# Routed attention and a token/channel mixer on one core: half sums of the exponentials added on VectorE, denominators a unit later, and another row for the stored weights

## The chip, the cores and the metric

The kernel runs on one core of a Trainium2 chip. The core has a matrix engine (TensorE, PE in the profile, with its weight loads shown as PEld), VectorE (DVE), ScalarE (ACT), GpSimd (POOL) and SyncE (SP), which here only issues transfers. Transfers are carried by 16 DMA engines. Working data lies in one SBUF tile named `arena`; TensorE writes into PSUM, the tile `ps` of eight banks. The metric is the time of one execution in microseconds on the device. Before the change its median is 799.9 us over three runs, which lay between 799.69 and 800.42.

## The reference

Everything is float32. Attention comes first, with 4 batches, 8 heads, 768 tokens and 64 values per head; a token sees only the tokens whose nearest centroid (of 16 for its head) is its own:

```python
q_assign = argmax(einsum('bhsd,hcd->bhsc', q_n, c_n), -1)   # the same for k
mask = q_assign[:, :, :, None] == k_assign[:, :, None, :]
scores = where(mask, scale * q @ k.T, -1e9)
attn = exp(scores - max(scores));  attn = attn / (sum(attn) + 1e-9)
x = (attn @ v)  # as (B, S, H*D) = (4, 768, 512)
```

Then a mixer over tokens and one over channels:

```python
h = maximum(x.T @ w_tok1, 0) @ w_tok2;   u = x + h.T
out = u + maximum(u @ w_ch1, 0) @ w_ch2    # 512 -> 1536 -> 512
```

The four weight matrices come as 8-byte floating point numbers, and the kernel itself turns them into float32.

## The kernel before

**The planner.** The program is not issued as it is written. Each operation is added to a `Program` (L74) with the engines that can do it, an estimated cost, and what it reads and writes. `run` (L117) gives each one a due time, worked back from the times at which PE would want its results, and `plan` (L148) then orders every engine's instructions: PE keeps the order in which its work was added, the other engines take, of what is ready, whatever is due first. `after` is the earliest time the plan may start an operation. The estimated costs stand in `COST` (L52) and the latency of transfers in `add` and `plan`. What comes out is a fixed order per engine; every engine then works in that order and waits for semaphores where it must. SP issues nearly all transfers, in one queue.

**Attention.** The 32 heads are done as 16 pairs. `pair(m)` (L1283) first runs `scores(m)` (L1148): twelve chunks, each of two score products (64 rows of the array each) plus two small products that add the mask, into two of the banks 0 to 5, and for each chunk one exponential on ACT (L1191) over 768 columns. The results lie in six buffers of a ring of seven (`exs`), each 128 x 1536. Then come the products with v (`values`, L1219, six per pair, each 16 small matrix products 32 columns wide) into banks 6 and 7, `route(m + 2, 0)` for a later pair's mask, and `sums(m, 5)` (L1233), which adds up the denominators over partitions.

The denominators are made in two steps. VectorE adds the six buffers by threes: two sums `es[0]` and `es[1]`, two adds each, every one of them 128 x 1536 (end of `scores`). Then `sums` multiplies both by a matrix of ones, four small products of 384 columns for each of the two, one accumulating onto the other in bank 5. `finish_x` (L1247) transposes the denominators out of bank 5 (L1250), keeps them in `dall`, takes reciprocals, transposes the products out of banks 6 and 7 (L1264) and multiplies. In PE's order `sums(m)` stands ahead of the last of the six `values` of the same pair.

Beside this, q and k are loaded, split into 16-bit halves by ACT (`part_qk`), transposed by DMA, and joined again by ACT (`join_qk`, L871).

**Weights.** During attention VectorE also rounds the weights from 8 bytes, in 31 pieces of up to 512 columns: `weight_round` (L1307), four instructions (L1327 to L1337) and an add. Piece n may be loaded from 14 + 11 n us of the plan on. `channel_weights` (L1384) handles the two big matrices: per slice s two pieces fill the first four of eight operands in `O`, VectorE makes the other four with `sub1`, and four more per slice with `sub2` into `Os`. These are the seven weight forms of Strassen's scheme in Winograd's variant, at two levels, which trades matrix products for additions. Seven stores per slice write them to scratch tensors in DRAM, `wd1` and `wd2`, in rows of 256 bytes (64 values), 224 KB each.

**Mixer.** The token stage (`token1`, `token2`) makes `uTs`, with VectorE adding each PE result of 384 columns. Then for each of two groups of batches `channel1` and `channel2` run seven products (`product`, L1671), each of seven weight forms. A weight form is 192 KB, loaded from `wd1` or `wd2` into one of eight `ring` buffers in rows of 1536 bytes, and used by three matrix products of 128 x 384. `weights_in_range` and `check` (L1872) count what tells whether a slower, more careful path would be needed (it isn't). `check` is written between the two groups: eight short VectorE instructions and a small matrix product.

Of the kernel before, what the change touches and what calls it, by code (L numbers as in the profile page):

```python
# [20 lines left out]
P = 128  # L21
# [28 lines left out]
GRAIN = 32  # L50

COST = {  # L52
    "ACT": (0.09, 0.00083),
    "ACT16": (-0.36, 0.001426),
# [12 lines left out]
START, STEP = 14, 11  # L67


class Op:  # L70
    __slots__ = ("opts", "fn", "preds", "succs", "left", "ready", "end", "due", "seq", "eng", "lat", "bytes", "after", "port", "first_lat", "mode", "early")


class Program:  # L74
# [10 lines left out]
    def add(self, opts, fn, rd=(), wr=(), size=None, after=0.0, mode=None, early=0.0):  # L85
# [3 lines left out]
        o.lat, o.mode, o.early = 0.0, mode, early  # L89

        o.port = not any(type(k) is tuple and k[0] == "ps" for k in list(rd) + list(wr))
        if size:
            o.bytes = BUS * size[0] / size[1] * (11 + 0.037 * size[1]) / 16e3
            o.lat = 5.0 + o.bytes / BUS
# [53 lines left out]
    def plan(self):  # L148
# [14 lines left out]
        while len(order) < len(ops):  # L163
# [39 lines left out]
            if o.bytes:  # L203
                bus = max(bus, o.end + 0.6) + o.bytes / BUS
                o.lat = bus + LAND - o.end
# [514 lines left out]
def kernel(  # L720
# [36 lines left out]
    wd1 = dram.tile([7, 7, P, 3 * P], F32, name="wd1")  # L757
    wd2 = dram.tile([7, 7, P, 3, P], F32, name="wd2")
# [45 lines left out]
    O = buf(119, [8, 2, 2, W])  # L804
# [62 lines left out]
    def halves(dst, src, n, rd, wr, engines=("ACT",)):  # L867

        def fn(e):
# [6 lines left out]
            {e: cost("ACT16" if e == "ACT" else e, n) for e in engines}, fn, rd, wr  # L876
# [17 lines left out]
    def vec(fn, c, rd, wr, early=0.0):  # L894
        return g.add({"DVE": c - 0.08}, lambda e: fn(), rd, wr, early=early)
# [8 lines left out]
    def transpose(dst, src, rd, wr, kb):  # L904
        return g.add(
            {"SP": ISSUE}, lambda e: nc.sync.dma_start(dst, src, transpose=True), rd, wr,
            (kb * 1024, 256),
# [150 lines left out]
    def join_qk(m):  # L1058
# [3 lines left out]
        for n in range(2):  # L1062
            for r in range(0, NQK, NJ):
                halves(
                    dst[:, r : r + NJ, :, n], qkt[n].ap[:, r : r + NJ], S,
                    qkt[n].k() + [("exps", m - 2)], T.rows(r, r + NJ),
# [81 lines left out]
    def scores(m):  # L1148
# [26 lines left out]
        for n in range(2 * NJ):  # L1175
# [21 lines left out]
            )  # L1197
        for n in range(2):
# [3 lines left out]
            tt(a.ap, a.ap, z.ap, ALU.add, 2 * S, a.k() + z.k(), a.k())  # L1202

# [29 lines left out]
    def sums(m, bk):  # L1233
        for n in range(2):
# [4 lines left out]
                        tokens(es[n].ap.rearrange("p h t -> p (h t)"), gr), n == 0, n == 1,  # L1239
# [7 lines left out]
    def finish_x(m, bk):  # L1247
        b, hp = divmod(m, H // 2)
        x, rcp = xs[b], rcps[m % 2]
        vec(lambda: nc.vector.transpose(out=denT.ap, in_=ps[:, bk, 0:HS]), 0.57, bank(bk), denT.k())  # L1250
        def den():
# [9 lines left out]
        cols = slice(hp * P, (hp + 1) * P)  # L1261
        xk = x.rows(0, NJ, hp * P, (hp + 1) * P)
        vec(
            lambda: nc.vector.transpose(  # L1264
                out=x.ap[:, :, cols].rearrange("p j (c d) -> p c j d", d=32),
                in_=ps[:, 6:8, 0:HS],
# [740 lines left out]
```

## Time and profile before

| What | Value |
|---|---|
| Median of three runs | 799.9 us |
| The profiled execution | 799.38 us, its span 797.6 us |
| PE busy | 783.8 us (98%) |
| DVE busy | 659.4 us (83%) |
| ACT busy | 469.8 us (59%) |
| POOL busy | 188.8 us (24%) |
| DMA | 143.69 MB in 264881 packets, mean 180 GB/s |

The profile is that of one execution. "Span" is the time from its first to its last instruction; the execution's own time has 1.8 us more around it. A row of instructions names the line of the kernel, the engine, the operation and what it writes and reads; many rows have a helper's line (L842 every single matrix product, L1208 the groups of small ones in `values` and `sums`, L881 every two-input add, L871 the 16-bit copies, L901 the transfers), so the shapes tell them apart. In the rows of a timeline the first two numbers are the start and the time from the start of the first to the end of the last instruction of the row, "x" is how many there are, and square brackets hold the idle time of the engine just before them, with what ended it. PE's matrix products overlap at their ends, so a row's time is longer than the distance from its start to the next row's. In the rows of stages, each engine's busy time is followed by its count of instructions; then come the clock granted to TensorE as a share of full speed, the busy share of the 16 DMA engines, and what they moved.

### The profile page before, as it was taken

Reading aid. Unit: us, or ns where it says so; the run is one execution under the profiler, and the core shown is the slowest. Engines: PE = TensorE matmul, PEld = TensorE weight load, DVE = VectorE, ACT = ScalarE, POOL = GpSimd, SP = SyncE. Lnnn points to the kernel's source line nnn. Section 1 sums busy time; section 2 is a strip of 40 time slices with the busy share of each in tenths; the row PEclk is TensorE's granted clock in tenths of the full one; section 3 lists DMA queues with packets and bytes.
Section 4 is the critical chain, followed back from the end, with each engine's and each line's share of the span. In section 5 each row is a group of like instructions: output and inputs, shape, how many; then the busy total and the mean of one; then the engine's idle time right before and its main releaser. Section 6 shows DMA issues by size and latency. Waiting matters only on the chain.

```text
span 797.6 us, 15467 instructions
## 1 busy us (share of the span) xinstructions
PE 783.8 (98%) x6063; PEld 466.9 (59%) x6063; DVE 659.4 (83%) x861; ACT 469.8 (59%) x618; POOL 188.8 (24%) x184
## 2 busy tenths in 40 slices
PE   7999999999999999999999999999999999999997
PEld 5566666666666666544555555555555555555554
DVE  6988899999999999999994677899952566799964
ACT  5588888888888875698714568503256104400433
POOL 0000000000000000000353499800186379840000
PEclk9999999999999999999999999999999999999999
DMA  9466779999999985479848787635597433333766
GB/s 213 153 160 167 172 169 229 223 211 215 229 226 237 223 249 134 97 148 211 177 122 274 270 290 265 223 99 144 143 210 195 130 106 102 99 104 105 177 148 154
DMA packets 264881, 143.69 MB, mean 180 GB/s; under 512 B 184160, under 2 KB 260704, under 8 KB 264800
## 3 DMA queue, kind: packets, MB, share of 16 engines
q1 hardware_dynamic: 262432, 141.83, 70.2%
q8 instruction: 50, 0.82, 0.4%
q10 hardware_dynamic: 2368, 0.79, 0.4%
q14 instruction: 31, 0.25, 0.1%
HBM read 91.95 MB, written 28.61 MB: 151 GB/s over the span
## 4 chain that ended last, share of the span: by engine, by line
PE 82%; DVE 11%; ACT 4%; issue 2%; ACTq 0%; DVEq 0%
PE ps L842 65%; PE ps L1208 17%; DVE arena L881 9%; ACT arena L871 3%; ACT arena L861 1%; ACT arena L888 0%; DVE arena L863 0%; DVE arena L1264 0%; DVE arena L1337 0%; ACTq L901 0%; ACT L980 0%; ACT arena L1191 0%; DVE arena L1334 0%; DVE arena L1331 0%; DVE arena L1086 0%
## 5 line engine op out<-in xcount | busy, mean ns | idle before, releaser
L842 PE MATMUL ps<-arena 128*128 128x384 f32 (+5 forms) x2735 | 639.7, 462 | 8.4 <-DVE arena L881 2.1
L842 PEld LDWEIGHTS ps<-arena 128*128 128x128 f32 (+1 forms) x2351 | 341.1, 184 | 252.0 <-issue 62.7
L881 DVE TENSOR_TENSOR arena<-arena 128x1536 f32<-128x1536 f32 (+6 forms) x341 | 354.8, 1063 | 19.8 <-ACT arena L1191 9.0
L881 POOL TENSOR_TENSOR arena<-arena 128x384 f32<-128x384 f32 x178 | 188.1, 1086 | 516.5 <-DVE arena L881 382.4
L881 DVE TENSOR_TENSOR arena<-ps,arena 128x384 f32<-128x384 f32 (+3 forms) x227 | 189.3, 844 | 100.2 <-PE ps L842 90.4
L871 ACT COPY arena<-arena 128x768 uint16<-128x768 uint16 x223 | 192.0, 952 | 58.7 <-DVE arena L881 29.3
L1191 ACT ACTIVATE arena<-ps 128x768 f32<-128x768 f32 x192 | 153.8, 810 | 30.4 <-PE ps L842 29.3
L1208 PE MATMUL ps<-arena 128*32 128x192 f32 (+1 forms) x3328 | 151.1, 339 | 0.0
L1208 PEld LDWEIGHTS ps<-arena 128*32 128x32 f32 x3328 | 106.5, 110 | 48.0 <-issue 18.3
L861 ACT COPY arena<-ps 128x1152 f32<-128x1152 f32 (+2 forms) x45 | 32.8, 738 | 133.7 <-PE ps L842 125.2
L888 ACT ACTIVATE arena<-arena 128x1152 f32<-128x1152 f32 (+1 forms) x38 | 40.0, 1077 | 55.8 <-DVE arena L881 55.3
L1865 ACT ACTIVATE arena<-arena 128x768 f32<-128x768 f32 x40 | 38.5, 967 | 17.3 <-DMA arena<-in_moe_w_ch_dram 17.0
L842 PEld LDWEIGHTS <-arena 64*128 64x128 bf16 x384 | 19.2, 94 | 25.0 <-issue 0.6
L1095 ACT ACTIVATE arena<-arena 128x384 bf16<-128x384 f32 x16 | 11.3, 707 | 16.3 <-issue 9.9
L1331 DVE SCALAR_TENSOR_TENSOR arena<-arena 128x512 uint32<-128x512 uint32 (+1 forms) x31 | 20.5, 667 | 0.5
L1337 DVE SCALAR_TENSOR_TENSOR arena<-arena 128x512 f32<-128x512 uint32 (+1 forms) x31 | 20.3, 666 | 0.5
L1264 DVE STREAM_TRANSPOSE arena<-ps 128x768 f32<-128x768 f32 x16 | 15.6, 974 | 0.6 <-PE ps L1208 0.4
L1327 DVE TENSOR_SCALAR arena<-arena 128x512 uint32<-128x512 uint32 (+1 forms) x31 | 12.6, 406 | 0.3 <-DMA arena<-in_moe_w_ch_dram 0.3
L1334 DVE TENSOR_SCALAR arena<-arena 128x512 uint32<-128x512 uint32 (+1 forms) x31 | 12.3, 409 | 0.4
L1086 DVE STREAM_TRANSPOSE arena<-ps 128x384 f32<-128x384 f32 x16 | 9.2, 575 | 3.0 <-PE ps L842 2.7
L1250 DVE STREAM_TRANSPOSE arena<-ps 128x384 f32<-128x384 f32 x16 | 9.2, 575 | 0.8 <-PE ps L1208 0.6
L1091 DVE STREAM_TRANSPOSE arena<-arena 128x384 f32<-128x384 f32 x16 | 9.3, 578 | 0.6
(58 smaller groups left out, 47.2 us busy)
## 6 DMA issues: line engine op xcount, KB each, us to landing
arena<-wd SPq DMA_DIRECT2D x196, 192.0 KB, 2.4
wd<-arena SPq DMA_DIRECT2D x84, 224.0 KB, 3.6
arena<-in_moe_w_ch_dram SPq DMA_DIRECT2D x48, 256.0 KB, 4.6
arena<-in_moe_w_ch_dram SPq DMA_DIRECT2D x16, 768.0 KB, 5.3
arena<-in_v_dram SPq DMA_DIRECT2D x16, 384.0 KB, 4.8
out_dram<-arena SPq DMA_DIRECT2D x14, 384.0 KB, 4.1
arena<-in_k_dram SPq DMA_DIRECT2D x13, 384.0 KB, 4.0
arena<-in_q_dram SPq DMA_DIRECT2D x13, 384.0 KB, 4.4
```

What stands on the lines that cost most here:

```text
L842: nc.tensor.matmul(dst, lhsT=lhsT, rhs=rhs, start=start, stop=stop, tile_position=pos, is_transpose=tr, skip_group_check=True,)
L861: nc.scalar.copy(out=dst, in_=src)
L871: nc.scalar.copy(out=dst, in_=src)
L881: (nc.vector if e == "DVE" else nc.gpsimd).tensor_tensor(out=dst, in0=a, in1=b, op=op)
L888: nc.scalar.activation(out=dst, in_=src, func=ACT.Relu)
L1191: lambda e, ex=ex, s=s, u=u: nc.scalar.activation(out=ex.ap[:, :, u * HS : (u + 1) * HS], in_=ps[:, 2 * s : 2 * s + 2, 0:HS], func=ACT.Exp ...
L1208: nc.tensor.matmul(dst, lhsT=lhsT, rhs=rhs, start=start, stop=stop, tile_position=pos, skip_group_check=True,)
L1264: lambda: nc.vector.transpose(out=x.ap[:, :, cols].rearrange("p j (c d) -> p c j d", d=32), in_=ps[:, 6:8, 0:HS],),
L1327: vec(lambda: nc.vector.tensor_scalar(out=hh, in0=hi, scalar1=0x07FFFFFF, scalar2=3, op0=ALU.bitwise_and, op1=ALU.logical_shift_left,), f, ...
L1331: vec(lambda: nc.vector.scalar_tensor_tensor(out=TT, in0=hi, scalar=0xC0000000, in1=hh, op0=ALU.bitwise_and, op1=ALU.bitwise_or), 0.14 + 0 ...
L1337: vec(lambda: nc.vector.scalar_tensor_tensor(out=ll, in0=lo, scalar=float(2.0**-52), in1=hh.bitcast(F32), op0=ALU.mult, op1=ALU.mult,), 0. ...
L1865: lambda e, i=i, func=func, bias=bias, n=n, hi=hi: nc.scalar.activation(out=hi, in_=hi, func=func, bias=bias, accum_out=wsum.ap[:, i, n : ...
```

## The change

Five things are changed.

- For the pairs 1 to 10 (`FOLD`), VectorE adds `es[0]` to `es[1]`, one more add of 128 x 1536, and `sums` multiplies only `es[1]`: four small products in place of eight. The other six pairs are as before.
- The four adds (and the fifth) are taken out of `scores` into `add_up`, and `sums(m - 1)`, the denominators' part of `finish_x(m - 1)` and `add_up(m)` are now written in pair m after the first of its `values`. The last pair's `sums` stands behind its `values`, in bank 4.
- The operands of the weights are laid out so that the seven forms of a slice lie side by side. A store writes a row of 1792 bytes per partition into the new tensors `wds`, and a ring load gathers its six pieces of 256 bytes per partition. For that the raw weights are loaded in four transfers a piece rather than two, in rows of 512 bytes as before.
- The eight VectorE instructions of `check` may not be placed before 532 us of the plan.
- Constants of the planner: a piece of weights may be loaded from 14 + 10 n us on; the cost of 16-bit copies is set 0.085 us higher, for the joining ones 0.195 us; DMA transposes are counted 1.5 us later.

The core of the diff:

```diff
+CHECK_AT = 532.0
+FOLD = "-VVVVVVVVVV-----"
-    "ACT16": (-0.36, 0.001426),
+    "ACT16": (-0.275, 0.001426),
+    "JOIN16": (-0.165, 0.001426),
-START, STEP = 14, 11
+START, STEP = 14, 10
...
-            o.lat = 5.0 + o.bytes / BUS
+            o.lat = 5.0 + more + o.bytes / BUS
...
-    wd1 = dram.tile([7, 7, P, 3 * P], F32, name="wd1")
-    wd2 = dram.tile([7, 7, P, 3, P], F32, name="wd2")
+    wds = [dram.tile([7, P, 6, 7, W], F32, name=f"wd{i}") for i in (1, 2)]
...
-    O = buf(119, [8, 2, 2, W])
+    O = buf(119, [2, 2, 8, W])
...
+    def add_up(m):
+        st = unit[m]
         for n in range(2):
             a = es[n]
             x, y, z = st[HJ * n : HJ * n + HJ]
             tt(a.ap, x.ap, y.ap, ALU.add, 2 * S, x.k() + y.k(), a.k())
             tt(a.ap, a.ap, z.ap, ALU.add, 2 * S, a.k() + z.k(), a.k())
+        a, b = es[1], es[0]
+        if FOLD[m] == "V":
+            tt(a.ap, a.ap, b.ap, ALU.add, 2 * S, a.k() + b.k(), a.k())
...
     def sums(m, bk):
-        for n in range(2):
+        first = 0 if FOLD[m] == "-" else 1
+        for n in range(first, 2):
...
-                        tokens(es[n].ap.rearrange("p h t -> p (h t)"), gr), n == 0, n == 1,
+                        tokens(es[n].ap.rearrange("p h t -> p (h t)"), gr), n == first, n == 1,
...
-            if i == NJ - 1:
-                sums(m, 5)
+            if i == 1:
+                if m:
+                    sums(m - 1, 5)
+                    finish_x(m - 1, 5, 1)
+                add_up(m)
             values(m, i)
-        finish_x(m, 5)
+        if m == NP - 1:
+            sums(m, 4)
+        finish_x(m, 5, 0)
+        if m == NP - 1:
+            finish_x(m, 4, 1)
...
-                if which == 1:
-                    d = wd1[:, pn, :, W * s : W * (s + 1)]
-                else:
-                    c, hf = divmod(s, 2)
-                    d = wd2[:, pn, :, c, W * hf : W * (hf + 1)]
-                dma(d.rearrange("o p c -> p o c"), src, rd, [("wd", which, pn, s)],
-                    224, 4 * W)
+                dma(wds[which - 1][pn, :, s], src, rd, [("wd", which, pn, s)], 224, 28 * W)
...
-            src = wd1[qi, pn] if wide else wd2[qi, pn].rearrange("p a c -> p (a c)")
             dma(
-                w.ap.rearrange("p a c -> p (a c)"), src,
-                [("wd", which, pn, s) for s in range(6)], w.k(), 192, 1536,
+                w.ap.rearrange("p a (b c) -> p (a b) c", c=W), wds[which - 1][pn, :, :, qi],
+                [("wd", which, pn, s) for s in range(6)], w.k(), 192, 256,
             )
...
+        def late(fn, c, rd, wr, early=0.0):
+            return vec(fn, c, rd, wr, early, CHECK_AT)
```

In `finish_x` part 0 is the transpose out of banks 6 and 7, part 1 all that concerns the denominators and the final multiplication. In `channel_weights` and `weight_round_split` the views are rearranged for the new order of `O`; the number of instructions and of columns in each stays as it was.

120 lines of the change are left out of this document (65 added, 55 removed).

## The prediction

> **What bounds the kernel now.** I read the page first: busy time by engine, and the chain that ended last.
>
> ```profile
> PE 783.8 (98%) x6063; PEld 466.9 (59%) x6063; DVE 659.4 (83%) x861; ACT 469.8 (59%) x618; POOL 188.8 (24%) x184
> PEclk9999999999999999999999999999999999999999
> PE 82%; DVE 11%; ACT 4%; issue 2%; ACTq 0%; DVEq 0%
> ```
>
> PE leaves only 797.6 - 783.8 = 13.8 us idle, at full clock: time falls by PE work that goes, and rises by what makes PE wait. So I next asked for busy time by stage; the attention pairs lie in the first two rows and end at 333.
>
> ```profile
> core 0: us, PE busy (x) PEld busy (x) DVE busy (x) ACT busy (x) POOL busy (x), PEclk, DMA share, GB/s
> 20.00:140.00 120.00, 118.51 (x1730) 74.23 (x1728) 104.48 (x142) 98.55 (x131) 0.00 (x0) 1.00 0.71 176
> 140.00:320.00 180.00, 180.00 (x2608) 112.43 (x2606) 174.22 (x252) 146.71 (x189) 0.00 (x0) 1.00 0.91 216
> 340.00:380.00 40.00, 39.39 (x99) 18.23 (x98) 35.91 (x65) 37.87 (x52) 2.36 (x3) 1.00 0.87 181
> 380.00:418.00 38.00, 36.53 (x111) 20.01 (x110) 37.32 (x68) 18.01 (x20) 17.23 (x16) 1.00 0.66 147
> 418.00:440.00 22.00, 21.82 (x69) 12.59 (x68) 10.22 (x13) 10.84 (x17) 7.91 (x8) 1.00 0.82 267
> 440.00:480.00 40.00, 40.00 (x126) 23.52 (x125) 27.80 (x22) 24.34 (x45) 29.85 (x31) 1.00 0.83 287
> 580.00:620.00 40.00, 40.00 (x126) 23.41 (x125) 15.30 (x21) 24.12 (x27) 27.85 (x27) 1.00 0.88 203
> ```
>
> In 140-320 DVE's idle time is 5.78 us over 252 instructions, 23 ns each: full. It is nearly full again in 380-418 (37.32 of 38), where alone PE waits for it repeatedly, as PE's timeline shows:
>
> ```profile
> 400.92 6.72 PE L842 MATMUL ps<-arena 128*128 128x384 f32 x20 [0.90 <-DVE arena L881]
> 408.12 11.23 PE L842 MATMUL ps<-arena 128*128 128x384 f32 x34 [0.48 <-DVE arena L881]
> 419.53 20.91 PE L842 MATMUL ps<-arena 128*128 128x384 f32 x64 [0.18 <-DVE arena L881]
> ```
>
> That is 1.56 us. The change takes work from the first bound and adds to the second; that is the whole question.
>
> **The sums on PE.** One pair's second half, in PE's timeline (128x192 are `values`, the 8 at L842 `route`, and the last 80 hold `sums` and two `values`):
>
> ```profile
> 284.84 5.41 PE L1208 MATMUL ps<-arena 128*32 128x192 f32 x128
> 290.06 0.83 PE L842 MATMUL ps<-arena 128*32 128x384 f32 x8
> 290.71 4.07 PE L1208 MATMUL ps<-arena 128*32 128x192 f32 x80
> 294.71 9.96 PE L842 MATMUL ps<-arena 64*128 64x384 f32 x72
> ```
>
> From 284.84 to 290.06 run four `values`: 5.22 / 4 = 1.305 each. From 290.71 to 294.71 run two and a `sums`: 4.00 - 2.61 = 1.39 with the change of tile shape at its end. By columns a `sums` (8 x 384) equals a `values` (16 x 192), so I take 1.305; half goes in ten pairs: 10 x 0.65 = **-6.5 us** (bounds -6.4 and -7.0). PE never waits in these pairs, so all of it shortens the path.
>
> **The adds on VectorE.** Its groups by shape, 20 to 340 us:
>
> ```profile
> L881 DVE TENSOR_TENSOR arena<-arena 128x1536 f32<-128x1536 f32 x70 | 122.5, 1757 | 12.8 <-ACT arena L1191 9.0 <-DVE arena L881 0.5
> L881 DVE TENSOR_TENSOR arena<-arena 128x448 f32<-128x448 f32 x36 | 21.8, 617 | 0.0
> L881 DVE TENSOR_TENSOR arena<-arena 128x512 f32<-128x512 f32 x22 | 15.0, 687 | 0.5
> L1331 DVE SCALAR_TENSOR_TENSOR arena<-arena 128x512 uint32<-128x512 uint32 x22 | 14.8, 683 | 0.3
> L1337 DVE SCALAR_TENSOR_TENSOR arena<-arena 128x512 f32<-128x512 uint32 x22 | 14.6, 681 | 0.3
> L881 DVE TENSOR_TENSOR arena<-arena 128x256 f32<-128x256 f32 x36 | 14.1, 417 | 0.5
> L1327 DVE TENSOR_SCALAR arena<-arena 128x512 uint32<-128x512 uint32 x22 | 9.1, 413 | 0.3 <-DMA arena<-in_moe_w_ch_dram 0.3
> L1334 DVE TENSOR_SCALAR arena<-arena 128x512 uint32<-128x512 uint32 x22 | 8.9, 418 | 0.2
> ```
>
> Ten more adds of 128x1536 are 10 x 1.757 = 17.6 us, and attention is 6.5 us shorter: 24.1 us of DVE time to find. Idle before 140 is 120 - 104.48 = 15.5 us, less 142 x 0.023 = 3.3 for gaps: 12.2 us. STEP 10 reaches it in part. A weight piece is 0.413 + 0.683 + 0.418 + 0.681 + 0.687 = 2.88 us, and two pieces share 4 x 0.417 + 4 x 0.617 = 4.14 us of subtractions: 4.95 a piece. By 140 us, 126/10 - 126/11 = 1.15 more pieces are released, 5.7 us. So 24.1 - 5.7 = 18.4 us slides behind attention (at least 24.1 - 12.2 = 11.9). What slides should be rounding, which the planner's due times put behind whatever PE waits for. Where it can go, from VectorE's timeline:
>
> ```profile
> 394.01 0.41 DVE L1327 TENSOR_SCALAR arena<-arena 128x512 uint32<-128x512 uint32 x1
> 423.04 0.25 DVE L1877 TENSOR_SCALAR arena<-arena 128x192 f32<-128x192 f32 x1
> 431.51 1.36 DVE L881 TENSOR_TENSOR arena<-ps,arena 128x1152 f32<-128x1152 f32 x1 [7.06 <-PE ps L842]
> ```
>
> The last piece starts at 394; behind 418 DVE idles 11.8 us to 440 and 12.2 to 480, and the check at 423 (held back to 532) leaves about 1 more: 25 us for 18.4. How late may it go? Each channel-1 product multiplies 7 ring loads, one per 1.91 us (worked out below), so 13.4 us; the add at 431.51 is the fourth result of the second product. Channel 2 starts five products after its end, past 500. But `raws` and `tmps` lie under the tile of `Hs` that the fourth product writes first, at 431.5 - 3 x 1.91 + 2 x 13.4 = 452.6, or 446 when all comes 6 us sooner: rounding must be done by then, the subtractions may be later. It fits, without much room. Full VectorE cost PE 1.56 us in one 38-us stretch; this one is fuller, and I take **+1.0 us** more (bounds -1.5, those waits gone, and 18.4, none absorbed).
>
> Rounding that slides runs beside POOL; the same 128x384 add there, 380 to 420:
>
> ```profile
> L881 DVE TENSOR_TENSOR arena<-arena 128x384 f32<-128x384 f32 x6 | 4.6, 812 | 0.0
> ```
>
> [...]
>
> ```profile
> 454.16 26.03 POOL L881 TENSOR_TENSOR arena<-arena 128x384 f32<-128x384 f32 x27 [2.26 <-DVE arena L881]
> ```
>
> **Denominators a unit later.** `sums(m-1)` now stands one `values` into the next second half and overwrites bank 5, which the last exponential reads.
>
> ```profile
> 205.78 5.41 PE L1208 MATMUL ps<-arena 128*32 128x192 f32 x128
> 205.95 0.81 ACT L1191 ACTIVATE arena<-ps 128x768 f32<-128x768 f32 x1
> ```
>
> That exponential ends at 206.76; `sums` would start at 205.78 + 1.305 = 207.09. The 0.33 us must cover the handoff, which from PE to ACT takes 0.17 here. Zero, bounds 0 and 15 x 0.2 = +3. The fold has a whole unit (19 us) before `sums` wants it, where its four adds now have under half of one. The WAR on `es` holds the first adds of the unfolded pairs until `sums(m-1)` is through; the buffers they free are wanted some 8 us on. In pair 15 the four adds (7.0 us) start about 2 us into the second half and `sums(15)` comes after 1.3 + 6 x 1.305 = 9.1: zero, up to +1.
>
> **Rows of 1792 bytes.** 84 stores shrink from 896 packets to 128, 196 ring loads grow from 128 to 768. The DMA answers for 660-700 (ring loads alone), 365-392 (nearly all 256-byte packets), and the first 15 us (mostly 256-byte loads):
>
> ```profile
> q1 hardware_dynamic: 2929, 3.99, 34.7%
> arena<-wd SPq DMA_DIRECT2D x21, 192.0 KB, 2.3
> ...
> q1 hardware_dynamic: 18454, 4.84, 91.5%
> ...
> q1 hardware_dynamic: 7594, 3.04, 91.4%
> ```
>
> A ring load takes 0.347 x 40 / 21 = 0.66 us of all 16 engines. A 256-byte packet takes 0.915 x 27 x 16 / 18454 = 21.4 ns, at most 28.9 by the last row: 768 / 16 of them are 1.03 us (1.39). PE uses one load per 40 / 21 = 1.91 us. Tightest is 580-620, DMA at 0.88: without ring loads 0.53, then 0.53 + 21 x 1.03 / 40 = 1.07 (1.26), so DMA falls 2.8 to 10.4 us behind; the ring is 8 x 1.91 = 15 us deep, loads landing in 2.3. Zero, bounds 0 and +3. SP issues twice as many raw loads (96 for 48) and takes longer over each ring load: hidden in the ring's depth. The cheaper stores cover nothing on the path and are worth zero.
>
> **The check, costs and latency constants.** Eight short VectorE instructions, under 2 us, find room in 532-600; PE's one matmul of them near 600 waits if they are late (0 to +2, taken 0). The planner's constants only reorder: 0, within 1 either way.
>
> **Sum.** The profiled execution took 799.38 us (span 797.6): 799.4 - 6.5 + 1.0 = 793.9. It stood 0.5 below the median of 799.9, so 794.4.
>
> **Rivals.** *A, VectorE's overflow sets the end* (slower). If weight work keeps its place ahead of the 384-wide adds until 418, PE waits for whatever exceeds DVE's idle 4.1 + 0.7 there. It decides at 6.5 + 4.8 = 11.3 us of the 18.4; with 14 ahead 9.2 us are waited: about 802.5. For it: the 1.56 us, and the pieces at 394 inside that stretch. Against: those pieces ran there because nothing forced them later.
> *B, the last exponential* (slower). The group of ACT's 16-bit copies, and the blocks of exponentials in its timeline (first and last of 13 whole ones):
>
> ```profile
> L871 ACT COPY arena<-arena 128x768 uint16<-128x768 uint16 x223 | 192.0, 952 | 58.7 <-DVE arena L881 29.3
> ...
> 58.67 9.75 ACT L1191 ACTIVATE arena<-ps 128x768 f32<-128x768 f32 x12 [1.59 <-PE ps L842]
> ...
> 295.83 9.75 ACT L1191 ACTIVATE arena<-ps 128x768 f32<-128x768 f32 x12 [1.61 <-PE ps L842]
> ```
>
> If ACT puts one copy (0.95 us) ahead of the last exponential, each `sums` waits 0.6: 15 x 0.6 = 9 us, 803. It decides at 0.43 per pair beyond the 0.33. Against: all twelve of a pair stand in one block, with no copy between.
> [...]
> *D, no effect:* the saving and waits cancel, 800.
>
> **Chances.** Forecast 0.70 (its own range 792.2 to 797.5: -7.0 with waits gone, to +4 of waits), A 0.13, B 0.06, C 0.04, D and smaller sums near 800 0.07. Differences under 0.2% (1.6 us) can't be told from none: faster 0.72, same 0.05, slower 0.23. The range 792.0 to 802.0 takes in half of A and leaves the rest out.
>
> **What would show it.** Right: the 128*32 128x384 form at L1208 falls by 80 of 256, pairs 2 to 11 turn in 19.1 us instead of the (295.83 - 58.67) / 12 = 19.76 of the blocks above, no wait on L1191 at PE; DVE busy in 418-440 near 18 us; PE idle in 380-420 below 4 us. Wrong: PE waiting for VectorE over 6 us between 360 and 445 (A), PE idle at every `sums` (B), ring loads landing beyond 10 us (C).

## The result and the profile after

The changed kernel takes 794.09 us (median; 793.79 to 794.77), against 799.8 us (799.66 to 800.42) for the kernel before beside it. The ratio is 0.9929 [0.9917, 0.9941]: 0.7% faster. Timed again beside the experiments, the kernel before took 799.4 to 801.2 us in 56 of 58 executions and 807.5 and 807.7 us in two, of which there is no profile. The forecast was 794.4 us. The profiled execution took 794.77 us, its span is 793.0 us. In the lines below line numbers are those of the changed kernel: L844 is every single matrix product, L1226 `values` and `sums`, L883 the two-input adds, L1193 the exponentials, L1097 the activation that makes a pair's mask in `route`, L1088 the first VectorE step of `route`, L1356 to L1366 a weight piece, L903 the transfers.

The page of the changed kernel: busy time, granted clock, and the chain that ended last.

```profile
PE 780.1 (98%) x5983; PEld 465.4 (59%) x5983; DVE 677.5 (85%) x876; ACT 461.2 (58%) x612; POOL 190.2 (24%) x185
PEclk9999999999999999999999999999999999999999
PE 88%; DVE 5%; ACT 3%; issue 2%; DMA 1%; SPq 0%; POOL 0%; DVEq 0%; POOLq 0%; ACTq 0%
```

80 rows of matrix products fewer (the profile shows each of the 40 products that are gone as two), and VectorE 18 us busier: the exchange that was meant. PE still has 12.9 us of idle time, and the chain runs through PE for 88% in place of 82%.

The stages of the changed kernel (columns as in the prediction: busy time and count of each engine, clock, DMA share, GB/s):

```profile
20.00:140.00 120.00, 118.43 (x1708) 74.38 (x1706) 107.94 (x140) 99.53 (x133) 0.00 (x0) 1.00 0.72 178
140.00:320.00 180.00, 179.80 (x2596) 111.96 (x2598) 172.27 (x244) 145.88 (x193) 0.00 (x0) 1.00 0.72 195
380.00:418.00 38.00, 37.11 (x111) 20.43 (x111) 35.95 (x61) 15.72 (x18) 18.74 (x18) 1.00 0.65 154
418.00:440.00 22.00, 22.00 (x70) 12.96 (x69) 21.18 (x26) 11.09 (x16) 8.98 (x8) 1.00 0.89 272
440.00:480.00 40.00, 40.00 (x126) 23.51 (x125) 31.10 (x30) 21.15 (x35) 32.08 (x33) 1.00 1.06 286
```

VectorE, which had 11.8 us free in 418 to 440 before, is now full there (21.18 of 22), and yet PE waits for nothing. In 380 to 418 PE's idle time went from 1.47 to 0.89 us. The busy share of the DMA engines reads 1.06 in 440 to 480, where it was 0.83, again with no wait of PE.

One folded pair and the scores behind it, in PE's timeline:

```profile
86.58 6.05 PE L1226 MATMUL ps<-arena 128*32 128x192 f32 x136
92.44 0.83 PE L844 MATMUL ps<-arena 128*32 128x384 f32 x8
93.09 2.78 PE L1226 MATMUL ps<-arena 128*32 128x192 f32 x64
95.80 10.15 PE L844 MATMUL ps<-arena 64*128 64x384 f32 x72
105.89 6.05 PE L1226 MATMUL ps<-arena 128*32 128x192 f32 x136
```

From 86.58 to 95.80 is 9.22 us, where the pair quoted in the prediction took 294.71 - 284.84 = 9.87: 0.65 us less, to the hundredth the price that was forecast. But the 72 score products take 10.15 us, not 9.96. ACT's timeline beside it shows why, and VectorE's shows what came before:

```profile
96.92 6.52 ACT L1193 ACTIVATE arena<-ps 128x768 f32<-128x768 f32 x8 [2.65 <-PE ps L844]
103.34 0.70 ACT L1097 ACTIVATE arena<-arena 128x384 bf16<-128x384 f32 x1
103.94 0.19 ACT L1097 ACTIVATION_READ_ACCUMULATOR arena<-arena 128x1 f32 x1
104.03 2.90 ACT L1193 ACTIVATE arena<-ps 128x768 f32<-128x768 f32 x4
```

```profile
89.70 5.30 DVE L883 TENSOR_TENSOR arena<-arena 128x1536 f32<-128x1536 f32 x3
94.92 0.58 DVE L1088 STREAM_TRANSPOSE arena<-ps 128x384 f32<-128x384 f32 x1
```

`route`'s products on PE end at 93.1, its VectorE steps begin at 94.92 behind three large adds, and so its mask activation on ACT comes too late for the gap ahead of the exponentials: it stands between the eighth and the ninth. The last chunks' exponentials are 0.9 us late, and PE waits 0.2 us for a free bank. This happens in seven of the ten folded pairs, which turn in 19.31 us; the other three turn in 19.12. The list of waits from 57 to 255 has it as one row (total, times and longest, of the weight loads), which the kernel before does not have:

```profile
PEld ps L844 <- ACT arena L1193: 3.3, 7, 0.5
```

Times of one and the same matrix product in both traces tell where the gain arises. The first score product starts at 10.01 us before and at 11.00 after: 0.99 us later, in a stretch that the change does not touch (last section). Without that, the changed kernel is ahead by 6.26 us at pair 12, 5.78 at pair 14, 4.49 when attention ends, 5.37 at the first product of channel 1, and 5.74 at the end, and 5.7 is also the difference of the medians.

### The profile page after: what moved, and what is told of

Same layout as the page of the kernel before. It is cut to its first block, busy times and chain, and to the rows that moved or that the text cites. A ratio compares the mean times of both kernels' runs of the same rounds, so it can differ in the third digit from the quotient of the medians.

```text
span 793.0 us, 15364 instructions
## 1 busy us (share of the span) xinstructions
PE 780.1 (98%) x5983; PEld 465.4 (59%) x5983; DVE 677.5 (85%) x876; ACT 461.2 (58%) x612; POOL 190.2 (24%) x185
## 4 chain that ended last, share of the span: by engine, by line
PE 88%; DVE 5%; ACT 3%; issue 2%; DMA 1%; SPq 0%; POOL 0%; DVEq 0%; POOLq 0%; ACTq 0%
PE ps L844 72%; PE ps L1226 16%; DVE arena L883 4%; ACT arena L873 2%; DMA wd<-arena 1%; ACT arena L1193 1%; DVE arena L865 0%; DVE arena L1360 0%; SPq L903 0%; DVE arena L1363 0%; ACT arena L863 0%; DVE arena L1366 0%; DVE arena L1356 0%; DVE arena L1280 0%; DVE arena L1273 0%
## 5 line engine op out<-in xcount | busy, mean ns | idle before, releaser
L844 PE MATMUL ps<-arena 128*128 128x384 f32 (+5 forms) x2735 | 642.4, 463 | 7.3 <-DVE arena L865 2.7
L844 PEld LDWEIGHTS ps<-arena 128*128 128x128 f32 (+1 forms) x2351 | 342.3, 185 | 252.8 <-issue 59.5
L883 DVE TENSOR_TENSOR arena<-arena 128x1536 f32<-128x1536 f32 (+6 forms) x350 | 370.2, 1079 | 10.5 <-PE ps L1226 2.3
L883 POOL TENSOR_TENSOR arena<-arena 128x384 f32<-128x384 f32 x179 | 189.5, 1094 | 510.8 <-DVE arena L883 379.4
L883 DVE TENSOR_TENSOR arena<-ps,arena 128x384 f32<-128x384 f32 (+3 forms) x227 | 189.6, 845 | 79.4 <-PE ps L844 75.4
L873 ACT COPY arena<-arena 128x768 uint16<-128x768 uint16 x221 | 189.4, 953 | 61.4 <-DMA arena<-arena 31.9
L1193 ACT ACTIVATE arena<-ps 128x768 f32<-128x768 f32 x192 | 150.6, 811 | 31.6 <-PE ps L844 29.9
L1226 PE MATMUL ps<-arena 128*32 128x192 f32 (+1 forms) x3248 | 144.7, 335 | 0.0
L1226 PEld LDWEIGHTS ps<-arena 128*32 128x32 f32 x3248 | 103.8, 110 | 44.0 <-issue 13.9
L863 ACT COPY arena<-ps 128x384 f32<-128x384 f32 (+2 forms) x41 | 29.5, 728 | 120.6 <-PE ps L844 120.4
L844 PEld LDWEIGHTS <-arena 64*128 64x128 bf16 x384 | 19.3, 94 | 25.0 <-issue 0.6
L1360 DVE SCALAR_TENSOR_TENSOR arena<-arena 128x512 uint32<-128x512 uint32 (+1 forms) x31 | 20.6, 681 | 0.3
L1097 ACT ACTIVATE arena<-arena 128x384 bf16<-128x384 f32 x16 | 11.2, 703 | 16.1 <-issue 16.1
L1366 DVE SCALAR_TENSOR_TENSOR arena<-arena 128x512 f32<-128x512 uint32 (+1 forms) x31 | 20.2, 671 | 0.4
L1356 DVE TENSOR_SCALAR arena<-arena 128x512 uint32<-128x512 uint32 (+1 forms) x31 | 13.2, 435 | 5.8 <-DMA arena<-in_moe_w_tok_dram 5.8
L1363 DVE TENSOR_SCALAR arena<-arena 128x512 uint32<-128x512 uint32 (+1 forms) x31 | 14.4, 483 | 0.3
L865 DVE COPY arena<-ps 128x384 f32<-128x384 f32 (+3 forms) x12 | 8.0, 666 | 4.7 <-PE ps L844 4.6
L1088 DVE STREAM_TRANSPOSE arena<-ps 128x384 f32<-128x384 f32 x16 | 9.2, 575 | 3.1 <-PE ps L844 3.0
```

Source lines behind the costliest of these rows:

```text
L844: nc.tensor.matmul(dst, lhsT=lhsT, rhs=rhs, start=start, stop=stop, tile_position=pos, is_transpose=tr, skip_group_check=True,)
L863: nc.scalar.copy(out=dst, in_=src)
L873: nc.scalar.copy(out=dst, in_=src)
L883: (nc.vector if e == "DVE" else nc.gpsimd).tensor_tensor(out=dst, in0=a, in1=b, op=op)
L1193: lambda e, ex=ex, s=s, u=u: nc.scalar.activation(out=ex.ap[:, :, u * HS : (u + 1) * HS], in_=ps[:, 2 * s : 2 * s + 2, 0:HS], func=ACT.Exp ...
L1226: nc.tensor.matmul(dst, lhsT=lhsT, rhs=rhs, start=start, stop=stop, tile_position=pos, skip_group_check=True,)
```

## The experiments

Line numbers in rows of kernels built on the old one are the old ones (L842, L881, L901). Where the times of a kernel lie far apart, a long wait of PE, named with it, need not occur in each of its executions. "The same product" means a comparison of start times as just above, less the difference at the first score product.

**All but the fold.**

```diff
-FOLD = "-VVVVVVVVVV-----"
+FOLD = "----------------"
```

> The changed kernel with no pair folded: every sums keeps its eight products and VectorE makes no fifth add; the deferral, the rows, the earlier pieces, the held-back check and the constants stay. My theory: the half sums are the whole gain, 6.5 us of PE work, of which about 1.4 us is lost again in seven pairs where the mask's activation now stands among the exponentials; without the fold this activation goes back ahead of them. So 794.1 + 6.5 - 1.4 = 799.2 us. Rival (the other parts carry part of the gain, by relieving DMA or by better constants): 795 to 797.5.

Measured: 797.64 us (797.16 to 797.79), ratio to the kernel before 0.9969 [0.9957, 0.998]. So the rest of the change is worth about 2.5 us on its own, and the fold 3.55 of the 5.7. By the same product this kernel is 0.12 us behind when attention ends, 1.51 ahead at channel 1 and 2.51 ahead near the end. The changed kernel gains 1.25 from the end of attention on, this one 2.63: there the fold costs 1.4 us. The theory had taken the rest of the change for nothing and missed; the rival's upper bound lies 0.14 us below the median.

**The fold alone**, in the kernel before:

```diff
+        if 1 <= m <= 10:
+            tt(es[1].ap, es[1].ap, es[0].ap, ALU.add, 2 * S, es[1].k() + es[0].k(), es[1].k())
...
-        for n in range(2):
+        for n in range(1 if 1 <= m <= 10 else 0, 2):
```

> The kernel before with one thing added: the fifth add and the half sums in pairs 1 to 10, sums still in its own pair ahead of the last values. My theory: the gain needs none of the other parts where VectorE can finish five adds in time. After the last exponential (0.98 us into the second half) three adds are left, 5.3 us, and sums comes at 5.2 + 0.65 + 1.3 = 7.2 us, so it fits and PE still saves 6.5 us: 793 to 795. Rival (the denominators must come a unit later, or VectorE's extra 17.6 us without the earlier pieces falls on the token stage): PE waits 0.5 to 1 us at each folded sums or 5 us behind attention: 798 to 803.

Measured: 802.37 us (796.27 to 809.87), ratio 1.0013 [0.9994, 1.0031]. By pair 12 it is ahead by the whole 6.25 us: the denominators need not come a unit later for this, the fifth add fits into the same pair. Nine of its ten folded pairs turn in 19.12 us, against three in the changed kernel, and pair 13 in 19.76, against 20.24. All is lost again from 473 us on (start, time, engine):

```profile
467.08 10.62 POOL L881 TENSOR_TENSOR arena<-arena 128x384 f32<-128x384 f32 x11
473.14 5.05 DVE L881 TENSOR_TENSOR arena<-arena 128x448 f32<-128x448 f32 x1
479.56 0.98 PE L842 MATMUL ps<-arena 128*128 128x384 f32 x1 [3.86 <-issue]
```

A subtraction of weight work, 617 ns in the prediction's rows, takes 5.05 us: it ends at 478.19, 0.49 us after GpSimd's unbroken row of adds. Behind it on VectorE stand the adds that empty PE's banks, and PE waits. The time is the rival's, and the loss lies behind attention as it said, but in channel 1 and not in the token stage. In this kernel weight work runs past 470 us; in the changed one the last subtraction ends at 450.4.

**Route earlier**, to bring the mask activation ahead of the exponentials:

```diff
-            if i == 4 and 1 <= m < NP - 2:
+            if i == 2 and 1 <= m < NP - 2:
```

> The changed kernel with route for a later pair two values earlier in the second half. My theory: its mask activation then stands ahead of the twelve exponentials in every pair from the second on, as before the change, and PE no longer waits 0.20 us for exponentials in seven of the folded pairs, nor about 0.5 us in pair 13: 794.1 - 1.4 - 0.5 = 792.2. Rival (the waits come from the sums now standing behind the first values, or from ACT being full at the shorter pair): no gain, 794.1.

Measured: 809.35 us (808.64 to 809.69), ratio 1.0115 [1.01, 1.013]. Both missed. Two places earlier `route` needs k before ACT has joined its halves (L873, 57 to 330 us); pairs turn in 20.6 us:

```profile
PEld ps L844 <- ACT arena L873: 17.0, 23, 0.8
PE ps L844 <- ACT arena L873: 3.9, 10, 0.4
```

This says nothing on the cause of the 0.2 us; it shows that `route` cannot be had earlier on PE.

**The old rows**, 256-byte stores and ring loads of 1536 bytes, in the changed kernel:

```diff
-                dma(wds[which - 1][pn, :, s], src, rd, [("wd", which, pn, s)], 224, 28 * W)
+                dma(d.rearrange("o p c -> p o c"), src, rd, [("wd", which, pn, s)], 224, 4 * W)
...
-                [("wd", which, pn, s) for s in range(6)], w.k(), 192, 256,
+                [("wd", which, pn, s) for s in range(6)], w.k(), 192, 1536,
```

> The changed kernel with the stored weights as before: stores in rows of 256 bytes, ring loads in rows of 1536 bytes; all else as changed. My theory: no transfer of weights is on PE's path either way, so 794.1 within 0.7. Rival one (the new rows relieve the DMA where it was full, 140 to 320 us, and carry part of the gain): 795.5 or more. Rival two (ring loads of 256 bytes delay something behind 560 us): 793 or less.

Measured: 798.48 us (797.97 to 799.0), ratio 0.9979 [0.997, 0.9988]. That is the rival's number, but no transfer stands on PE's path. PE's timeline, then VectorE's:

```profile
404.13 2.20 PE L845 MATMUL ps<-arena 128*128 128x384 f32 x6 [2.67 <-DVE arena L884]
```

```profile
403.19 0.42 DVE L1357 TENSOR_SCALAR arena<-arena 128x512 uint32<-128x512 uint32 x1
403.52 0.55 DVE L884 TENSOR_TENSOR arena<-ps,arena 128x384 f32<-128x384 f32 x1
403.99 0.68 DVE L1361 SCALAR_TENSOR_TENSOR arena<-arena 128x512 uint32<-128x512 uint32 x1
404.71 0.43 DVE L1364 TENSOR_SCALAR arena<-arena 128x512 uint32<-128x512 uint32 x1
405.08 0.56 DVE L884 TENSOR_TENSOR arena<-ps,arena 128x384 f32<-128x384 f32 x1
```

With other costs of transfers the planner draws up another order, and a weight piece stands between the adds that PE waits for: rival A's mechanism. What the rows themselves are worth cannot be read from a run in which the order changes with them; that stays open.

**A fence behind route.** The adds of a pair's second half, the fifth with them, are issued after `route` and made to depend on its last VectorE step:

```diff
+                add_up(m, 1, rt[2].k() if 1 <= m < NP - 2 else [])
...
-            tt(a.ap, x.ap, y.ap, ALU.add, 2 * S, x.k() + y.k(), a.k())
+            tt(a.ap, x.ap, y.ap, ALU.add, 2 * S, x.k() + y.k() + after, a.k())
```

> Edit: the adds of a pair's second half, the fifth among them, are issued after route and made to depend on the last tile that route's VectorE steps write, so that no 128x1536 add can stand between route's products and its mask activation. Theory (in seven of the ten folded pairs the mask activation stands behind the eighth exponential because route's VectorE step waited behind a 128x1536 add; scores take 10.15 us instead of 9.96 there, 1.4 us in all, and one mask pair more in pair 13, 0.5): the activation stands ahead of all twelve exponentials again, scores take 9.96 us in every pair, and the time is 794.1 - 1.9 = 792.2 us. Rival (the fifth add costs this much wherever it is put, because VectorE is full): another wait of PE takes its place, 793.8 us or more.

Measured: 813.08 us (801.75 to 815.11), ratio 1.011 [1.0045, 1.0175]. In attention the theory holds: scores take 9.96 us, and by pair 12 the kernel is 7.62 us ahead, 1.36 more than the changed one. Then it loses 11 us between 470 and 515, as the next run does.

**STEP 11 again**, in the changed kernel:

```diff
-START, STEP = 14, 10
+START, STEP = 14, 11
```

> Edit: the changed kernel with STEP 11 again, so that weight pieces are released as late as before. Theory (what ruined the fold alone was weight work left over when GpSimd works without a gap from 454 us on; releasing pieces earlier is the part of the change that prevents it): weight work ends 5 to 15 us later than the 450 us of the changed kernel, VectorE's adds of 128x448 beside GpSimd take several us, PE waits for them, 797 to 803 us with a spread of some us. Rival (STEP carries nothing, the check held back and the constants do it): 794 to 795 us, with weight work done by about 450 us.

Measured: 803.24 us (798.94 to 814.9), ratio 1.0012 [0.9983, 1.0042], as the theory had it. The way there was not quite the one expected. Weight work ends at 499 us, 49 us later, not 5 to 15, and the subtractions beside GpSimd take 0.6 to 1.4 us here, not several. What strikes is SP's queue (its timeline; then PE's, then the stage):

```profile
493.62 2.51 SPq L903 DMA_DIRECT2D wd<-arena  x2
496.92 4.30 SPq L903 DMA_DIRECT2D arena<-wd  x2
501.31 0.59 SPq L903 DMA_DIRECT2D wd<-arena  x1
501.99 1.96 SPq L903 DMA_DIRECT2D arena<-wd  x3
```

```profile
514.46 10.80 PE L844 MATMUL ps<-arena 128*128 128x384 f32 x27 [5.49 <-DMA arena<-wd]
```

```profile
500.00:520.00 20.00, 14.51 (x40) 8.14 (x39) 12.58 (x12) 11.08 (x18) 13.55 (x10) 0.83 0.88 246
```

The stores of the last weights stand among the ring loads in one queue. The loads behind them come late, PE waits 5.49 us, and the clock reads 0.83 from 500 to 520 us and 1.00 from 520 to 560. The fence has the same order of stores, its queue waits 3.6 us for a store to land between 470 and 520, and PE waits 5.82 us at the same place; the clock of 500 to 520 is 0.84 there.

**The fold with STEP 10**, nothing else:

```diff
-START, STEP = 14, 11
+START, STEP = 14, 10
```

> Edit: the kernel before with the fifth add in pairs 1 to 10 and sums over one tile there (as in the fold alone), and STEP 10; denominators stay in their own pair, rows, check and constants are the old ones. Theory (the release of weight pieces was what the fold alone lacked): 794.5 to 796 us and a spread below 1 us; weight work is over by about 455 us. Rival (the denominators a unit later, the check held back or the constants are needed too): 798 to 803 us, again with a spread of several us.

Measured: 810.19 us (809.56 to 811.42), ratio 1.0109 [1.0068, 1.015]. The theory fell in its price: weight work is over by 449 us, as it had foreseen, and the kernel is slower all the same, in each of its six executions. At 462 us the check of counts, which is not held back in this kernel, takes 11.96 us in its first instruction (the rows of such a case are shown with the check not held back, below). PE waits 10.72 us.

**The planner's old figures**, in the changed kernel:

```diff
-    "ACT16": (-0.275, 0.001426),
-    "JOIN16": (-0.165, 0.001426),
+    "ACT16": (-0.36, 0.001426),
+    "JOIN16": (-0.36, 0.001426),
...
-            (kb * 1024, 256), more=1.5,
+            (kb * 1024, 256),
```

> Edit: the changed kernel with the planner's old figures for ACT's 16-bit copies (-0.36 for -0.275 and -0.165) and without the 1.5 us more for transposing loads. Theory (the stages behind attention gained about 2 us without the fold, and it is the order that the new figures give there that brought it): 795.5 to 796 us. Rival (they only reorder work that is hidden, as the prediction had it): 794.1 us, within 0.5.

Measured: 797.8 us (797.26 to 800.2), ratio 0.9964 [0.9942, 0.9986]. The constants are no nothing: 3.7 us by the medians, 2.9 by the spans (795.9 and 793.0). The theory had the mechanism and too small a size. From the end of attention to the end of the kernel it loses 1.60 us where the changed kernel gains 1.25. PE's waits from 325 to 420 (total, times, longest):

```profile
PE ps L844 <- ACT arena L890: 1.8, 1, 1.8
PE ps L844 <- DVE arena L883: 1.7, 3, 0.8
```

In the changed kernel PE waits there for VectorE 0.9 us in all and for ACT 0.2.

**The fence with earlier weights:**

```diff
-START, STEP = 14, 10
+START, STEP = 8, 9
```

> Edit: as in the fence (the adds of a pair's second half made to depend on route's last VectorE step), with START 8 and STEP 9, so that weight pieces are released earlier; the planner then puts the last subtraction behind 14 of VectorE's 1152-wide adds of channel 1, as in the changed kernel, and not behind 39 as in the fence. Theory (the mask activation is worth 1.4 to 1.9 us, and the fence lost its gain through the weight work that ran on beside GpSimd, not through the fence): 792.2 us, within 0.6, and a spread below 1 us. Rival (the fence itself makes PE wait somewhere else): 794 us or more.

Measured: 792.94 us (792.71 to 793.24), ratio 0.9911 [0.9899, 0.9924]: faster than the kernel before, 1.15 us below the median of the changed kernel, and just beyond the 0.6 allowed. The intervals of the two ratios overlap, but the times of the two kernels do not, and by the same product it is 1.17 us ahead of the changed one near the end. PE's and ACT's timeline in the pair shown above:

```profile
95.22 9.96 PE L844 MATMUL ps<-arena 64*128 64x384 f32 x72
```

```profile
95.55 0.71 ACT L1097 ACTIVATE arena<-arena 128x384 bf16<-128x384 f32 x1 [1.94 <-issue]
96.17 0.19 ACT L1097 ACTIVATION_READ_ACCUMULATOR arena<-arena 128x1 f32 x1
96.33 9.76 ACT L1193 ACTIVATE arena<-ps 128x768 f32<-128x768 f32 x12
```

The mask activation stands ahead of all twelve exponentials and the scores take 9.96 us. By the same product pairs 2 to 11 gain 1.36 us over the changed kernel and pair 13 0.48, which are the 1.4 and 0.5 of the theory; 0.5 is given back in pairs 0 and 1, where weight work now begins earlier.

**Four more pairs folded**, with the fence and START 10:

```diff
-FOLD = "-VVVVVVVVVV-----"
-START, STEP = 14, 10
+FOLD = "-VVVVVVVVVVVVVV-"
+START, STEP = 10, 10
```

> Edit: the fence with pairs 1 to 14 folded and START 10; the last subtraction stands behind 8 of VectorE's 1152-wide adds of channel 1. Theory (each further pair gives 0.65 us of PE, and VectorE's 4 x 1.76 us more are found as long as weight work is over before GpSimd works without a gap): 792.2 - 4 x 0.65 = 789.6 us. Rival (VectorE is now too full, and PE waits for it between 360 and 420 us): 792 us or more.

Measured: 805.11 us (804.15 to 805.87), ratio 1.0062 [1.005, 1.0075]. The theory fell, and so did its premise: in the trace the last subtraction stands behind 39 of VectorE's 1152-wide adds, not 8, and ends at 504.8 us, as late as in the fence and with STEP 11. Attention ends 3.0 us earlier than in the fence with earlier weights (4 x 0.65 is 2.6), and from 402 us on 14.4 us are lost against it, 9.2 of them by 456. PE's timeline, and VectorE's ahead of it:

```profile
444.86 4.14 PE L844 MATMUL ps<-arena 128*128 128x384 f32 x12 [0.72 <-DVE arena L883]
452.95 19.16 PE L844 MATMUL ps<-arena 128*128 128x384 f32 x54 [3.96 <-issue]
```

```profile
448.83 0.69 DVE L1362 SCALAR_TENSOR_TENSOR arena<-arena 128x512 uint32<-128x512 uint32 x1
449.56 1.10 DVE L1365 TENSOR_SCALAR arena<-arena 128x512 uint32<-128x512 uint32 x1
450.69 0.69 DVE L1368 SCALAR_TENSOR_TENSOR arena<-arena 128x512 f32<-128x512 uint32 x1
451.49 1.36 DVE L883 TENSOR_TENSOR arena<-ps,arena 128x1152 f32<-128x1152 f32 x1
```

PE goes on at 452.95, when the add of 451.49 has emptied its bank, behind a whole weight piece. The planner's order is fixed: work that overflows does not slide behind what is urgent, PE slides with it. This is the mechanism of rival A and of this run's own rival, for the most part later than either had it. The losses behind 456 fall where those of the fence do (PE waits 2.03 us for a ring load at 514.07 and 1.33 us for VectorE at 519.50). So this run does not tell what 14 folds would give if weight work were over in time.

**The check not held back**, in the changed kernel:

```diff
-CHECK_AT = 532.0
+CHECK_AT = 0.0
```

> Edit: the changed kernel with CHECK_AT 0, so that the check of counts isn't held back; the planner then puts it behind 21 of VectorE's 1152-wide adds of channel 1, where GpSimd works without a gap. Theory (GpSimd's unbroken run of adds locks VectorE out of a single short instruction until it ends, 11.96 us for one of 128x192 in the fold with STEP 10): one instruction of the check lasts 8 us or more, PE waits 8 to 11 us, the clock falls after it, 803 to 812 us. Rival (what struck there came from the order of the kernel before, and the check is hidden as the prediction had it): 794.1 us, within 0.6.

Measured: 806.82 us (794.12 to 807.87): 12.7 us are lost by the medians, in five executions of six, and in one, of 794.12 us, nothing. That the stall belongs to the order of the kernel is shown by the fold with STEP 10, where it is as long, 11.96 us, and where all six executions lost. GpSimd, VectorE, PE, and the stage:

```profile
457.26 17.24 POOL L883 TENSOR_TENSOR arena<-arena 128x384 f32<-128x384 f32 x18
462.65 11.96 DVE L1903 TENSOR_SCALAR arena<-arena 128x192 f32<-128x192 f32 x1
475.94 6.26 PE L844 MATMUL ps<-arena 128*128 128x384 f32 x12 [10.72 <-DVE arena L883]
```

```profile
454.00:480.00 26.00, 15.28 (x42) 8.51 (x41) 21.11 (x9) 6.31 (x12) 20.50 (x22) 0.81 0.68 186
```

An instruction that takes 0.25 us where GpSimd is idle lasts 11.96 us, from 462.65 until GpSimd's row of adds ends at 474.50. In the fold with STEP 10, where the same happens, GpSimd's next add then waits 8.19 us for PE, which itself had waited for VectorE. PE waits 10.72 us, the clock is 0.81 over this stage, and by the same product the loss in this stretch is 13.1 us.

**The fold with STEP 10 and the check held back**, in the kernel before:

```diff
+        def late(fn, c, rd, wr, early=0.0):
+            return vec(fn, c, rd, wr, early, 532.0)
```

> Edit: the kernel before with the fifth add in pairs 1 to 10, sums over one tile there, STEP 10, and the check of counts held back to 532; denominators in their own pair, old rows, old figures of the planner. Theory (the lock-out of the check was all that the fold with STEP 10 lost): 810.2 - 14.3 = 795.9 us, within 1, spread below 1.5 us. Rival (the rest of the change is needed to keep PE fed there): 799 us or more, with a spread of some us.

Measured: 796.89 us (796.66 to 797.6), ratio 0.9962 [0.9949, 0.9974], as the theory had it. Three parts, the fold, the earlier release and the late check, make a kernel 3.2 us faster than before with times within 1 us; the fold without the other two or with STEP 10 alone did not (802.37 and 810.19). Later denominators, new rows and new figures are not needed for that; nine of its ten folded pairs turn in 19.12 us, as in the fold alone. By the same product it is 5.2 us ahead near the end, close to the changed kernel's 5.74. The rest of the difference lies behind the last matrix product: it starts at 786.70, and the span ends at 794.8, 8.1 us later; in the kernel before and in the changed one 5.7 and 5.8 us pass there (791.91 to 797.6, 787.15 to 793.0). The two other kernels made from the old one with the fold have these 8 us too (793.78 to 801.9, 800.88 to 808.8). What lengthens the end of the program there is open.

## Why the prediction was right, and where it was not

The sum came out: -6.5 + 1.0 = -5.5 forecast, -5.74 measured by the same product. That it is so near is in part luck: two terms that were put at 0 are wrong by 1.9 and 2.6 us, in opposite directions. By the runs it is -6.5 for the sums, +1.4 for VectorE, +1.9 for the denominators a unit later and -2.6 for the planner's constants, -5.8 in all. This is one way to split it, and the parts do not simply add up: the fold with STEP 10 and the late check has neither the later denominators nor the new figures, and stands at -5.2.

**The sums, -6.5: right.** 0.65 us in each folded pair, in the changed kernel as in the fold alone.

**VectorE's overflow, +1.0: right in size, shown only in part.** The fold costs 1.4 us from the end of attention on (2.63 gained without it, 1.25 with it). But PE's waits tell little of this: from 325 to 420 it waits for VectorE 0.9 us in the changed kernel and 0.7 without the fold, and for ACT 0.2 and 0. In 380 to 418, where the prediction looked for more waits than before, PE's idle time fell from 1.47 to 0.89 us. What the rest of the 1.4 us stands behind is open. How VectorE overflows was as told, only less slid:

```profile
L883 DVE TENSOR_TENSOR arena<-arena 128x1536 f32<-128x1536 f32 x79 | 137.2, 1746 | 5.1 <-PE ps L1226 2.3 <-ACT arena L1193 0.5 <-PE ps L844 0.2
L883 DVE TENSOR_TENSOR arena<-arena 128x448 f32<-128x448 f32 x32 | 19.2, 619 | 0.0
...
L1360 DVE SCALAR_TENSOR_TENSOR arena<-arena 128x512 uint32<-128x512 uint32 x20 | 13.3, 688 | 0.2
```

Between 20 and 340 us two pieces (22 to 20) and four of each subtraction (36 to 32) are missing: 2 x 2.88 + 4 x 0.617 + 4 x 0.417 = 9.9 us slid, not 18.4. Rounding ended at 436.9 us, ahead of the 446 to 452 that had been worked out as its limit, and the subtractions at 450.4. "It fits, without much room" was true: in the fence and with STEP 11 the subtractions ended 48 and 49 us later, and these kernels took 9 to 19 us more by the medians.

**The denominators a unit later, 0 (to +3): wrong, 1.9 us.** The step that failed is "PE never waits in these pairs, so all of it shortens the path", and with it the 0 of this term. The prediction looked at the handoff of bank 5, where PE waits for none of the `sums`, and rival B at a copy in the block of exponentials, and there is none. What got in was the mask activation of `route`, pushed back over VectorE by the adds that now stand in the same place of the pair: 7 x 0.2 us and 0.5 in pair 13. The fence gave 1.84 of it back. It takes both parts: with the later denominators and no fold the pairs lose nothing, and the kernels with the fold in its own pair lose 0.2 us of it. Beside this the later denominators move 1.3 us from pair 0 to pair 15.

**The planner's constants, 0 within 1: wrong, 2.6 us the other way.** The 2.6 us are what all the rest of the change gains behind attention without the fold. That the figures bring them is shown in the folded kernel alone, which with the old ones falls back by 2.85 us there. "Only reorder" is no price: the order decides whether PE waits 1.1 or 3.5 us between 325 and 420.

**The check, 0 (to +2): right for where it went, and blind to what it avoids.** The prediction priced moving the check to 532 and not leaving it at 423 while VectorE's work behind it grew. Left to the planner it slides to 462, and costs 12.7 us. In the traces an instruction of the check lasted 11.96 us and a subtraction 5.05 us, each to the end of GpSimd's whole row of adds, of which each takes 17.24 / 18 = 0.96 us in the row beside the check.

**STEP 10: undervalued.** It was counted as 5.7 us that find a place before 140. Taken back alone it costs 9.2 us by the medians (803.24 and 794.09), since it moves the end of weight work from 450 to 499.

**Rows, 0: right as far as PE goes.** Late ring loads (C of the chances) do not starve PE: with the DMA engines at 1.06 from 440 to 480, PE waits for no ring load. SP takes 0.52 us over a ring load (median) where it took 0.32, and the loads land in 3.0 us (median; 5.7 from 440 to 480) where they took 2.4. What the stores' fewer packets bring is not shown.

**The rivals.** A is real, one step off: its mechanism is seen in the run with the old rows (798.48) and in part of the loss with fourteen folds (805.11). Of the marks named beforehand, 80 rows of products fewer and PE idle below 4 us in 380 to 418 came (0.89); "no wait on L1191" did not; VectorE in 418 to 440 was put at 18 us and measured 21.18; pairs were put at 19.1 us, and seven of ten turn in 19.3.

## What to carry to other kernels

Trading matrix products for adds on a second engine is paid on PE to the hundredth (0.65 us a pair here), but whether it is kept hangs on what the added work pushes back: follow every instruction behind it, by its place in the order, to the stage where it lands, and price that stage. A fixed order does not let late work slide behind urgent work. A short instruction of VectorE on SBUF alone, of 0.25 us where GpSimd is idle, lasted 11.96 us here, to the end of an unbroken row of GpSimd adds; holding it back to where GpSimd is idle cost nothing here and was worth 12.7 us. A part that looks free has to be priced together with the others: the later denominators cost nothing in the pairs by themselves, and 1.9 us beside the fold. And where several edits go together, undo each one alone: here five of them lose 3.5 to 12.7 us each when taken back, far more together than the 5.7 us of the whole.

## What the runs showed of the hardware

**VectorE instructions that last to the end of GpSimd's row.** 0.25 us became 11.96 and 0.62 became 5.05, in each case to within 0.5 us of the end of GpSimd's row, while adds with one operand in PSUM kept their 1.36 us beside the same row. Other subtractions beside GpSimd took only 0.6 to 1.4 us, and one execution of the early check lost nothing. What decides between one instruction and the whole row is open.

**The clock after a wait.** Waits of PE of 5.49 and 10.72 us were followed by a granted clock of 0.83 and 0.81 in the stage. Behind the 10.72 us of the fold with STEP 10 it reads 0.50 from 470 to 480 us, and 7 products are counted in 4.49 us of busy time, where the changed kernel has 126 in 40 us, about 14 in 4.49. Behind the 10.72 us of the check not held back PE's weight loads start 0.64 us apart from 476.74 to 479.94, twice the 0.32 of the changed kernel (125 in 40 us). There this is about 2.4 us more on top of the 10.72. After a wait of 2.67 us (old rows) the clock of the stage stayed at 1.00, and the run with a wait of 1.78 (old figures) shows 0.998 as a whole, as the kernel before does.

**The start varies.** The first 45 products (128 x 128) start 213 ns apart at first and about 110 ns apart later. The switch came at 4.1 us in the profile of the kernel before and at 7.1 in that of the changed one, so that the 45 take 7.00 and 7.99 us; in three other profiles (no fold, the fold alone, the fence with earlier weights) they take 7.53, 7.00 and 7.07. It shows in the count of products from 4 to 6 us, in the kernel before and in the changed one, though the clock reads 1.00 in both:

```profile
4.00:6.00 2.00, 1.84 (x16) 1.65 (x15) 1.76 (x12) 1.12 (x2) 0.00 (x0) 1.00 1.30 231
```

```profile
4.00:6.00 2.00, 2.00 (x12) 2.00 (x11) 1.76 (x11) 1.12 (x2) 0.00 (x0) 1.00 1.32 234
```

This moves everything behind it by up to 1 us, as much as some of the effects above. The two profiles have the same start of products, 1.36 and 1.35 us, and switches 3.0 us apart; what sets the switch is not shown.
